# Reordering the prologue of a spectral-mixing and gated-FFN kernel: filter copies, first reads of D and A, and PE filler

## The chip, the cores and the metric

The kernel runs on one core of one Trainium2 chip. The metric is the time of one execution in microseconds of device time. Three runs of the kernel before gave 899.15, 899.78 and 900.06 us; the median is 899.78 us. One further execution was taken with the hardware profiler; it took 901.15 us, of which the profile's span covers 899.4 us.

## What is computed

Eight batches of 3008 x 256 numbers are filtered along the sequence in the frequency domain, and the result goes through a gated feed-forward layer:

```python
X = np.fft.rfft(x, axis=1)                        # x: (8, 3008, 256)
Y = X * (filt_r + 1j * filt_i)[None]              # filters: (1505, 256)
y = np.fft.irfft(Y, n=3008, axis=1).reshape(24064, 256)
gate = np.maximum(y @ w_gate, 0.0)                # 256 x 1536
out = (gate * (y @ w_val)) @ w_out                # 1536 x 256
```

## The kernel before

**Tiling of the transform.** A sequence of 3008 is treated as 94 x 32. Stage A is a DFT over the 94 (matmuls against the table `WA`), stage B a DFT over the 32 (table `F2`), then comes the product with the filters, the inverse of stage B (tables `I2t`, `I2u`) and the inverse of stage A (stage C, table `M1`). Between A and B and between the inverse of B and C the data has to change its layout. For batch 0 the first change is made on chip: `first_a` writes `AS`, and two VectorE transposes (`turn_a`, L292) make `AT`. For batch 1 it goes through HBM: `items_a(1)` makes sixteen items (four slabs c of four pieces j); an item is one float32 matmul (L304) and one eviction (L307), and each finished slab of four is stored to `Abuf` (L310); `load_at` reads it back as `at` in four transfers (L382). The second change goes through HBM for every batch: `inv` stores `Dbuf` (L445) and `load_d` reads `dC` (L471). From batch 2 on the items are made by a different path (`tiled_a`, table `WF`), which the change does not touch.

**Feed-forward blocks.** 24064 rows are cut into 47 blocks of 512. `item_c` makes the input of a block (`yT`) from `dC`; `gv` makes one of twelve pieces of gate and value (weights `WgT`, `WvT`, L510); `o_part` multiplies with `WoT` (L531), one block behind. The main loop runs `gv` and `o_part` and hangs the pieces of the next batches' transforms on numbered steps (`at_step`). The first of these, `fwd(1, 0)` at step 16, is the first reader of `at`.

**The prologue** is everything ahead of the main loop, and its order is written out by hand; each engine and each DMA queue executes in the order in which it is written. Three engines issue transfers: SP, ACT and POOL. POOL's transfers also convert float32 to bfloat16; filters and weights come in that way. An issuing engine waits in place for whatever its transfer needs, and everything written behind that transfer on the same engine waits with it.

The steps of the prologue that matter here, in the order of the code:

- `warm(n)` issues n matmuls on a tile of ones, `junk`, whose result nobody reads; it is filler for PE.
- `load_x(0, ...)` loads batch 0's x into `XF[0]` and `XF[1]` in column quarters of q = 1024 columns.
- `hold_gpsimd(tile)` is a tiny copy on POOL that makes POOL wait until a tile has landed. The first one stands ahead of `load_filters`, which loads the filters in two halves (groups 0 to 11, then 12 to 23), for `Ftr` and `Fti`, for two partition ranges a.
- `place_filter(fi, a, half, copy)` copies 32 partitions of a filter tile to the next 32 (L255). Eight such copies exist; one runs on POOL, seven are transfers on SP's queue.
- `load_x(1, ...)` loads batch 1's x over batch 0's, on SP's queue, when batch 0's stage A has read it.
- `first_b(amid)` runs the six steps i of batch 0's stage B: `fwd(0, i)`, four products, `inv(0, i-2)`, then `amid(i)`, which inserts filler and items of `items_a(1)` into PE's order. Products run on VectorE (L413) or, through a copy `xs` on ACT, on POOL (L411). PSUM has eight banks; `bank` hands them out in the order in which they were given back.
- After `first_b` come the first read of D for block 0 (`load_d(0, 0, 1, ...)`), the second half of the gate and value weights (`load_vg`), further reads of D, `load_o`, the rest of the items with `item_c(0, h)` in between, and `load_at(1, c)`.

The first read of D has two halves e, one on each of the two engines in `engs`. POOL waits for it with a second `hold_gpsimd`, so that the weights' second half starts behind it.

Of the kernel before, what the change touches and what calls it, by code (L numbers as in the profile page):

```python
# [35 lines left out]
def _ap(t, offset_elems, ap_list):  # L36
    return dataclasses.replace(
        t, offset=t.offset + offset_elems, ap=[list(p) for p in ap_list]
    )
# [81 lines left out]
def kernel(  # L121
# [10 lines left out]
    nc = tc.nc  # L132
# [11 lines left out]
    wa_h, fold_h, f2_h, tab_h = _tables()  # L144
# [8 lines left out]
    def bank(name, *shape):  # L153

        i = free.pop(0)
        t = ps.tile([128, *shape], FP32, tag=f"bank{i}", bufs=1, name=name)
        held[id(t)] = i, t
        return t

    def done(t):  # L160
        free.append(held.pop(id(t))[0])
# [7 lines left out]
    XF = [pro.tile([128, NX2 * D], FP32, name=f"XF{c}") for c in range(N2 // NX2)]  # L169
# [3 lines left out]
    WF = consts.tile([128, 4, 32], FP32)  # L173
# [11 lines left out]
    def load_x(b, engs, cols, ms=range(3)):  # L185
        w = NX2 * D
        for c, c0, c1 in cols:
            for m in ms:
                rows = min(32, B * N1 - (b * N1 + 32 * m))
                engs[m % len(engs)].dma_start(XF[c][m:m + 4 * rows - 3:4, c0:c1],  # L190
                              _ap(x, (b * N1 + 32 * m) * N2 * D + c * w + c0,
                                  [[N2 * D, rows], [1, c1 - c0]]))
# [38 lines left out]
    def load_filters():  # L231

        for g0 in (0, H):
            for src, dst in FILT:
                for a in range(2):
                    r, k1, n = a * 64, 1 + 24 * a + g0, H - (2 * a if g0 else 0)
                    nc.gpsimd.dma_start(dst[r:r + 31:2, g0:g0 + n, :],
                                        _ap(src, k1 * D, [[N1 * D, 16], [1, n * D]]))
                    nc.gpsimd.dma_start(dst[r + 1:r + 32:2, g0:g0 + n, :],
                                        _ap(src, (N1 - k1) * D, [[N1 * D, 16], [-D, n], [1, D]]))  # L240
            yield
# [8 lines left out]
    def place_filter(fi, a, half, copy):  # L250

        dst = FILT[fi][1]
        gs = slice(H * half, H * half + H)
        r = a * 64
        copy(dst[r + 32:r + 64, gs, :], dst[r:r + 32, gs, :])  # L255

    def place_nyq():
        for (src, dst), n in zip(FILT, nyq):
            nc.gpsimd.tensor_copy(dst[96:97, NG - 1, :], n)

    def load_vg(c0, c1):
        for (w_hbm, w_sb) in ((moe_w_val, WvT), (moe_w_gate, WgT)):
            nc.gpsimd.dma_start(w_sb[:, :, c0:c1],
                                _ap(w_hbm, c0, [[DFF, 128], [128 * DFF, 2], [1, c1 - c0]]))
# [7 lines left out]
    def hold_gpsimd(tile_):  # L272

        scr = sb.tile([128, 8], FP32, tag="scr", bufs=2)
        nc.gpsimd.tensor_copy(scr[:tile_.shape[0]], tile_)  # L275
# [19 lines left out]
    slabs = []  # L295

    def items_a(b):

        def one(c, j, st):
            if j == 0:  # L300
                st["asb"] = sb.tile([128, NC2 * D], BF16, tag="asb", bufs=4, name="asb")
            psA = bank("psA", 512)
            o = (c * NC2 % NX2) * D + j * 512
            nc.tensor.matmul(psA[0:NROW], WA[:, 128:], XF[c * NC2 // NX2][:, o:o + 512],  # L304
                             start=True, stop=True)
            copy = nc.vector.tensor_copy if c > 1 or (c, j) in ((0, 1), (0, 3)) else nc.scalar.copy
            copy(st["asb"][:NROW, j * 512:(j + 1) * 512], psA[0:NROW])  # L307
            done(psA)
            if j == 3:
                slabs.append(lambda: nc.sync.dma_start(  # L310
                    _ap(Abuf[b], c * NROW * NC2 * D, [[NC2 * D, NROW], [1, NC2 * D]]), st["asb"][:NROW]))
                if c != 1:
                    while slabs:
                        slabs.pop(0)()
        for c in range(N2 // NC2):
            st = {}
            for j in range(NC2 * D // 512):
                yield lambda c=c, j=j, st=st: one(c, j, st)
# [58 lines left out]
    ats = {}  # L377

    def load_at(b, c):
        if c == 0:  # L380
            ats[b] = sb.tile([128, NG, D], BF16, tag="at", bufs=1, name="at")
        nc.gpsimd.dma_start(ats[b][c:c + 125:4],  # L382
                          _ap(Abuf[b], c * NROW * NC2 * D, [[D, 32], [4 * NC2 * D, NG], [1, D]]))

    psXs, tus, dsbs, left = {}, {}, {}, {}
# [81 lines left out]
    def load_d(b, z0=0, z1=NZ, engs=(nc.sync, nc.sync)):  # L467
        for z in range(z0, z1):
            dC = sb.tile([NROW, 8, D], BF16, tag="dC", bufs=6)
            for e in range(2):  # L470
                engs[e].dma_start(dC[48 * e:48 * e + 48],  # L471
                                  _ap(Dbuf[b], (64 * e + 16 * z) * NG * D,
                                      [[D, 48], [48 * D, 8], [1, D]]))
            dCs[b, z] = dC
# [3 lines left out]
    def runs(t, n):  # L478

        o = 0  # L480
        while o < n:
            b, r = divmod(t + o, S)
            n2, n1 = divmod(r, N1)
            w = min(N1 - n1, n - o)
            yield o, b, n2, n1, w
            o += w

    def item_c(k, h):

        if h == 0:  # L490
            yTs[k] = sb.tile([128, 2, W], BF16, tag="yT", bufs=3, name="yT")
        psY = bank("psY", W)
        for (o, b, n2, n1, w) in runs(k * W, W):
            nc.tensor.matmul(psY[:, o:o + w],  # L494
                             dCs[b, n2 // 8][:, n2 % 8, h * 128:(h + 1) * 128], M1[:, n1:n1 + w],
                             start=True, stop=True)
        dst = yTs[k][:, h]
        if h == 0:
            nc.scalar.copy(dst, psY)  # L499
        else:  # L500
            nc.vector.tensor_copy(dst, psY)  # L501
        done(psY)
# [57 lines left out]
    junk = pro.tile([128, 512], BF16, tag="junk", bufs=1)  # L560

    def warm(n, cols=512):

        psJ = bank("psJ", 512)
        for i in range(n):
            nc.tensor.matmul(psJ[:, :cols], junk[:, 0:128], junk[:, :cols], start=True, stop=True)
        done(psJ)

    q = NX2 * D // 4
    both, sp = (nc.sync, nc.scalar), (nc.sync,)  # L570
    nc.sync.dma_start(WA, nc.inline_tensor(wa_h, name="dft_wa").ap())
    load_x(0, both, ((0, 0, q),), range(4))
    nc.vector.memset(junk, 1.0)
    nc.vector.memset(XF[0][:, q:2 * q], 0.0)
    nc.gpsimd.memset(XF[0][:, 2 * q:], 0.0)
    nc.vector.memset(XF[1][:, 0:2 * q], 0.0)
# [5 lines left out]
    for (src, dst) in FILT:  # L582
        nc.vector.memset(dst[64:128, NG - 2:, :], 0.0)
    filters = load_filters()
    hold_gpsimd(XF[1][:, 2 * q - 8:2 * q])
    next(filters)
    load_own_filters()
    next(filters)

    warm(6)  # L590
    for p, s, h in [(p, s, h) for p in range(2) for s in range(2) for h in range(2)]:
        first_a(p, s, h)
    for p, h in ((2, 0), (3, 0), (2, 1), (3, 1)):
# [9 lines left out]
    for i in range(6):  # L603
        warm(2)
    place_filter(1, 0, 0, nc.gpsimd.tensor_copy)
    for a in range(2):
        place_filter(0, a, 0, nc.sync.dma_start)
    place_filter(1, 1, 0, nc.sync.dma_start)
    load_x(1, sp, ((0, 0, 2 * q),))
    for fi in range(2):  # L610
        for a in range(2):
            place_filter(fi, a, 1, nc.sync.dma_start)
    load_x(1, sp, ((0, 2 * q, 4 * q),))

    early = items_a(1)

    def amid(i):
        if i == 3:
            place_nyq()
            load_vg(0, DFF // 2)  # L620
        if i == 3:
            load_x(1, sp, ((1, 0, 4 * q),))
        if i < 4:
            warm(2)
        for _ in range((0, 0, 0, 0, 1, 1, 1)[i]):
            next(early)()

    first_b(amid)
    load_d(0, 0, 1, (nc.scalar, nc.scalar))
    hold_gpsimd(dCs[0, 0][:, 7, D - 8:])  # L630
    load_vg(DFF // 2, DFF)
    load_d(0, 1, 2, (nc.gpsimd, nc.gpsimd))
    load_o()
    load_d(0, 2, 4, (nc.gpsimd, nc.gpsimd))
    nc.sync.dma_start(WF, nc.inline_tensor(fold_h, name="dft_fold").ap())
    for i, f in enumerate(early):
        f()
        if i == 9:
            for h in range(2):
                item_c(0, h)  # L640
    for c in range(4):
        load_at(1, c)
    prologue.close()
    fs = ctx.enter_context(tc.tile_pool(name="fs", bufs=2))
    XP = []
# [80 lines left out]
```

## Time and profile before

| what | value |
|---|---|
| median of three runs | 899.78 us (899.15 to 900.06) |
| profiled execution | 901.15 us, span 899.4 us |
| PE busy | 877.4 us, 98% of the span |
| VectorE, ACT, POOL busy | 573.0, 495.3, 379.0 us |
| mean granted PE clock | 0.989 |
| first `gv` matmul | 63.26 us after the span's start |
| first matmul on `at` | 83.32 us |

Times inside the profile are counted from the start of the span. In the views of DMA queues, q0 is POOL's queue, q1 is SP's and q10 is ACT's. A row of the view of windows gives the length of the window, each engine's busy time in it with the number of instructions in brackets, the PE clock that was granted (1.00 is full, 0.50 half), the share of the window in which the 16 DMA engines held packets (it can exceed 1, when several packets are under way at one engine), and GB/s. The two rows of the table on `gv` and `at` bracket the region that the change touches: the main loop behind it is the same code.

### The profile page before, as it was taken

How to read it: one execution, taken by the hardware profiler on the slowest of the kernel's cores; microseconds unless marked ns; L12 is line 12 of the kernel's file. 1: busy time of each engine (PE TensorE's matmuls, PEld its weight loads, DVE VectorE, ACT ScalarE, POOL GpSimd, SP SyncE). 2: the span in 40 equal slices, each digit the busy share in tenths (PEclk: the TensorE clock that was granted, in tenths of full speed). 3: DMA queues.
4: the chain of work that ended last, by engine and by line, in shares of the span. 5: the costliest groups of instructions: out<-in, count | busy, mean ns of one | idle time of the engine just before them, and what ended most of it. 6: DMA issues, size and time to landing. Idle time of an engine off the chain costs nothing.

```text
span 899.4 us, 19131 instructions
## 1 busy us (share of the span) xinstructions
PE 877.4 (98%) x7177; PEld 508.6 (57%) x7177; DVE 573.0 (64%) x868; ACT 495.3 (55%) x887; POOL 379.0 (42%) x378
## 2 busy tenths in 40 slices
PE   8788999999999999999999999999999999999997
PEld 3234564556555665566655566556655566666665
DVE  3646775667665776657766677656766577655553
ACT  5524665555655556555655565655565555555552
POOL 5624498118680386514773167701868000000001
PEclk9889999999999999999999999999999999999999
DMA  8897448443465344663355433753346512231111
GB/s 235 236 207 163 118 126 175 102 117 109 135 158 124 92 132 120 140 140 108 97 149 144 114 101 104 181 124 92 108 139 154 118 32 81 78 77 36 36 33 51
DMA packets 105810, 107.59 MB, mean 120 GB/s; under 512 B 20295, under 2 KB 89703, under 8 KB 105142
## 3 DMA queue, kind: packets, MB, share of 16 engines
q1 hardware_dynamic: 81126, 76.30, 32.9%
q0 software_dynamic: 23440, 29.16, 13.8%
q8 instruction: 56, 0.92, 0.4%
q10 hardware_dynamic: 1152, 0.92, 0.4%
q14 instruction: 36, 0.29, 0.1%
HBM read 60.55 MB, written 48.23 MB: 121 GB/s over the span
## 4 chain that ended last, share of the span: by engine, by line
PE 88%; DMA 7%; DVE 1%; issue 1%; SPq 1%; POOL 1%; ACT 0%; DVEq 0%; POOLq 0%; ACTq 0%
PE psV L510 26%; PE psO L531 26%; PE psG L510 25%; PE psF L354 3%; PE psD L434 2%; PE psY L494 2%; DMA at<-Abuf 2%; PE psX L397 2%; DMA dC<-Dbuf 2%; PE psA L283 1%; DVE AT L292 1%; DMA WvT<-in_moe_w_val_dram 1%; DMA Ftr<-Ftr 1%; DMA Abuf<-asb 1%; PE psA L304 1%
## 5 line engine op out<-in xcount | busy, mean ns | idle before, releaser
L515 DVE SCALAR_TENSOR_TENSOR prod<-psG,vsb 128x512 bf16<-128x512 f32 x564 | 388.7, 690 | 262.5 <-ACT vsb L513 254.9
L513 ACT CAST vsb<-psV 128x512 bf16<-128x512 f32 x564 | 332.1, 589 | 271.1 <-PE psV L510 228.4
L510 PE MATMUL psV<-yT,WvT 128*128 128x512 bf16 x1128 | 337.4, 380 | 0.6 <-DVE yT L501 0.6
L531 PE MATMUL psO<-WoT,prod 128*128 128x256 bf16 x2256 | 336.9, 273 | 0.0
L510 PE MATMUL psG<-yT,WgT 128*128 128x512 bf16 x1128 | 336.0, 380 | 0.0
L531 PEld LDWEIGHTS <-prod 128*128 128x128 bf16 x2256 | 221.0, 98 | 143.9 <-issue 0.8
L510 PEld LDWEIGHTS <-WgT 128*128 128x128 bf16 x1128 | 110.2, 98 | 135.0 <-issue 2.4
L510 PEld LDWEIGHTS <-WvT 128*128 128x128 bf16 x1128 | 98.6, 98 | 41.3 <-issue 30.1
L275 POOL CAST scr<-prod 128x8 f32<-128x8 bf16 x24 | 4.6, 190 | 248.3 <-DVE prod L515 248.3
L555 POOL DMA_DIRECT2D out_dram<-osb x5 | 2.6, 531 | 195.7 <-ACT osb L544 195.7
L413 DVE TENSOR_TENSOR tt<-psX,Ftr 128x512 bf16<-128x512 f32 x96 | 64.9, 680 | 6.2 <-PE psX L397 2.7
L544 ACT COPY osb<-psO 128x512 f32<-128x512 f32 x92 | 54.0, 586 | 26.6 <-PE psO L531 25.4
L340 POOL TENSOR_TENSOR fold<-XP 128x1024 f32<-128x1024 f32 x24 | 56.5, 2354 | 21.0 <-PE psF L354 18.9
L413 DVE TENSOR_TENSOR uu<-psX,Fti 128x512 bf16<-128x512 f32 x88 | 59.8, 679 | 2.4 <-DMA Fti<-Fti 2.4
L442 ACT CAST dsb<-psD 128x512 bf16<-128x512 f32 x94 | 50.5, 590 | 16.1 <-PE psD L434 16.1
L327 POOL DMA_DIRECT2D XP<-in_x_dram x96 | 57.7, 603 | 2.8 <-PE psY L494 1.5
L341 POOL TENSOR_TENSOR XP<-XP 128x1024 f32<-128x1024 f32 x24 | 56.3, 2348 | 2.0
L361 DVE CAST asb<-psF 128x512 bf16<-128x512 f32 x48 | 30.9, 686 | 18.5 <-PE psF L354 18.5
L361 ACT CAST asb<-psF 128x512 bf16<-128x512 f32 x48 | 25.8, 589 | 30.5 <-PE psF L354 30.5
L499 ACT CAST yT<-psY 128x512 bf16<-128x512 f32 x47 | 27.6, 586 | 25.7 <-PE psY L494 25.5
L494 PE MATMUL psY<-M,dC 96*128 96x94 bf16 (+18 forms) x604 | 38.1, 200 | 2.7 <-DMA dC<-Dbuf 2.7
L494 PEld LDWEIGHTS <-dC 96*128 96x128 bf16 x604 | 34.7, 98 | 7.1 <-issue 2.7
(75 smaller groups left out, 505.5 us busy)
## 6 DMA issues: line engine op xcount, KB each, us to landing
XP<-in_x_dram POOLq DMA_DIRECT2D x48, 256.0 KB, 6.1
Dbuf<-dsb SPq DMA_DIRECT2D x23, 512.0 KB
dC<-Dbuf SPq DMA_DIRECT2D x56, 192.0 KB
XP<-in_x_dram POOLq DMA_DIRECT2D x96, 96.0 KB, 2.7
Abuf<-asb SPq DMA_DIRECT2D x96, 96.0 KB
at<-Abuf SPq DMA_DIRECT2D x24, 384.0 KB
out_dram<-osb SPq DMA_DIRECT2D x69, 94.0 KB
XF<-in_x_dram SPq DMA_DIRECT2D x15, 256.0 KB
```

The costliest lines, as they stand in the source:

```text
L327: nc.gpsimd.dma_start(xp[r:r + 24, 0:4:2, :], _ap(x, (b * N1 * N2 + o) * D, [[N2 * D, 24], [47 * N2 * D, 2], [1, 512]]))
L340: tt(t, xp[:, 0:2], xp[:, 2:4], op=ALU.add)
L341: tt(xp[:, 2:4], xp[:, 0:2], xp[:, 2:4], op=ALU.subtract)
L361: copy(asf[:, :, q, :], banks[q])
L413: nc.vector.tensor_tensor(p, psX, filt, op=ALU.mult)
L442: copy(dsb[:, a, o:o + 2, :], psD[a])
L494: nc.tensor.matmul(psY[:, o:o + w], dCs[b, n2 // 8][:, n2 % 8, h * 128:(h + 1) * 128], M1[:, n1:n1 + w], start=True, stop=True)
L510: nc.tensor.matmul(pt[:, :W], w[:, h, ft * 128:(ft + 1) * 128], yt[:, h, :], start=(h == 0), stop=(h == 1))
L513: nc.scalar.copy(vsb, psV[:, :W])
L515: nc.vector.scalar_tensor_tensor(prod, in0=psG[:, :W], scalar=0.0, in1=vsb, op0=ALU.max, op1=ALU.mult)
L531: nc.tensor.matmul(psO[:, t % 2], prods[ft][:, t * 128:(t + 1) * 128], WoT[:, ft, :], start=(ft == 0), stop=(ft == NFT - 1))
L544: copy(osb[:, t0 % 2:t % 2 + 1], psO[:, t0 % 2:t % 2 + 1])
```

## The change

The edits, all in the prologue:

1. The filler ahead of `first_a` is 18 matmuls of 256 columns in place of 6 of 512, and the 256 columns of `junk` that these read are set by POOL; VectorE sets the other 256.
2. The first `hold_gpsimd` waits for the last columns of `XF[0]` in place of columns in the first half of `XF[1]`, which is the transfer group behind.
3. All seven filter copies on SP's queue are issued first, and then all of batch 1's x, without copies in between; the last third of x is no longer issued in `amid(3)`.
4. `amid` inserts 1, 2, 2 and 2 items at i = 3, 4, 5, 6 (before: 1 at 4, 5 and 6), and three filler matmuls at i = 0, 1, 2 (before: two at 0 to 3). The first half of the gate and value weights is issued at i = 5 in place of 3.
5. The first read of D has one half on SP's queue and the other on ACT's (before: both on ACT's), and the four stores to `Abuf` are issued behind it and behind all items, where before each went out when its slab was done.
6. `item_c(0, h)` stands ahead of the last two items in place of the last three.
7. `load_at` is issued on SP's queue in place of POOL's, and the table `WF` behind it.

```diff
@@ items_a
             if j == 3:
                 slabs.append(lambda: nc.sync.dma_start(... Abuf[b] <- asb ...))
-                if c != 1:
-                    while slabs:
-                        slabs.pop(0)()
@@ load_at
-        nc.gpsimd.dma_start(ats[b][c:c + 125:4],
+        nc.sync.dma_start(ats[b][c:c + 125:4],
@@ prologue
-    nc.vector.memset(junk, 1.0)
+    nc.gpsimd.memset(junk[:, 0:256], 1.0)
+    nc.vector.memset(junk[:, 256:], 1.0)
...
-    hold_gpsimd(XF[1][:, 2 * q - 8:2 * q])
+    hold_gpsimd(XF[0][:, 4 * q - 8:])
...
-    warm(6)
+    warm(18, 256)
...
     place_filter(1, 0, 0, nc.gpsimd.tensor_copy)
-    for a in range(2):
-        place_filter(0, a, 0, nc.sync.dma_start)
-    place_filter(1, 1, 0, nc.sync.dma_start)
-    load_x(1, sp, ((0, 0, 2 * q),))
-    for fi in range(2):
-        for a in range(2):
-            place_filter(fi, a, 1, nc.sync.dma_start)
-    load_x(1, sp, ((0, 2 * q, 4 * q),))
+    for fi, a, half in ((0, 0, 0), (0, 1, 0), (1, 1, 0), (0, 0, 1), (0, 1, 1), (1, 0, 1), (1, 1, 1)):
+        place_filter(fi, a, half, nc.sync.dma_start)
+    load_x(1, sp, ((0, 0, 2 * q), (0, 2 * q, 4 * q), (1, 0, 4 * q)))
@@ amid
         if i == 3:
             place_nyq()
+        if i == 5:
             load_vg(0, DFF // 2)
-        if i == 3:
-            load_x(1, sp, ((1, 0, 4 * q),))
-        if i < 4:
-            warm(2)
-        for _ in range((0, 0, 0, 0, 1, 1, 1)[i]):
+        if i < 3:
+            warm(3)
+        for _ in range((0, 0, 0, 1, 2, 2, 2)[i]):
             next(early)()
@@ behind first_b
-    load_d(0, 0, 1, (nc.scalar, nc.scalar))
+    load_d(0, 0, 1, (nc.sync, nc.scalar))
...
-    nc.sync.dma_start(WF, nc.inline_tensor(fold_h, name="dft_fold").ap())
     for i, f in enumerate(early):
         f()
-        if i == 9:
+        if i == 6:
             for h in range(2):
                 item_c(0, h)
+    for store in slabs:
+        store()
     for c in range(4):
         load_at(1, c)
+    nc.sync.dma_start(WF, nc.inline_tensor(fold_h, name="dft_fold").ap())
```

## The prediction

> **What bounds the kernel now.** I read the page first: 98% busy PE means that only waits of PE, and PE running at a low clock, can be won. So next comes the list of PE's waits over the whole span; its longest rows, with the span ahead of them:
>
> ```profile
> span 899.4 us, 19131 instructions
> PE psD L434 <- DVE uu L413: 4.3, 1, 4.3
> PE psY L494 <- DMA dC<-Dbuf: 2.7, 2, 1.5
> PE psX L397 <- DMA at<-Abuf: 2.6, 2, 2.1
> PE psA L304 <- ACT asb L307: 1.5, 1, 1.5
> ```
>
> The first three name the three handovers of the prologue: filters, first read of D, first read of A. Of the second and third, 1.1 and 2.1 us lie in the prologue. Third view, the chain that ended last, in order of time (start, length):
>
> ```profile
> 26.59 6.91 DMA Ftr<-Ftr
> 34.01 2.57 DMA Fti<-Fti
> 47.69 6.08 DMA Abuf<-asb
> 53.81 3.27 DMA dC<-Dbuf
> 57.66 7.21 DMA WvT<-in_moe_w_val_dram
> 74.54 8.65 DMA at<-Abuf
> ```
>
> From 26 to 83 us the end is carried by transfers, one after another. Fourth, windows around these waits:
>
> ```profile
> core 0: us, PE busy (x) PEld busy (x) DVE busy (x) ACT busy (x) POOL busy (x), PEclk, DMA share, GB/s
> 30.00:33.20 3.20, 2.40 (x38) 1.06 (x36) 1.49 (x3) 3.02 (x7) 2.92 (x4) 1.00 0.52 112
> 33.20:37.45 4.25, 0.00 (x0) 0.00 (x1) 1.44 (x3) 1.27 (x3) 1.24 (x2) 0.84 0.71 190
> 57.20:63.20 6.00, 5.99 (x18) 2.51 (x19) 2.06 (x3) 0.59 (x1) 5.73 (x9) 0.50 0.90 192
> 68.00:72.00 4.00, 4.00 (x25) 1.89 (x23) 3.26 (x5) 2.81 (x6) 1.91 (x3) 1.00 1.34 252
> 83.30:87.10 3.80, 3.78 (x19) 1.76 (x20) 1.98 (x3) 1.18 (x3) 0.00 (x0) 0.58 0.00 0
> ```
>
> Two things: a wait is paid twice, because PE then runs at half clock (0.50 after the read of D costs 3.0 us of 6.0; 0.58 after the read of A costs 1.6 of 3.8). And outside the gaps the DMA engines are full (0.90 to 1.34), so what is pulled forward pushes something back.
>
> **Filler and stage A of batch 0.** Before, filler runs 1.45 to 4.19 us, PE idles 0.96 until x lands, and the first evictions stand 1.71 us apart, later 0.86: two matmuls at half clock. Filler now has 4608 columns in place of 3072, 2.74 x 1.5 = 4.1 us, and starts after a POOL memset, at about 1.05; it closes the gap. Worth 0 to 1.7 us. Its cover is x, which lands at 5.0 anyway. Against it: the first hold on POOL was released at 12.24 by one group of x (0.79 MB; 303 GB/s in the window 5 to 12, so 2.6 us a group); now it is released a group earlier, near 9.65, and the filter loads run beside the last group. In the window 24 to 31, with both queues busy, SP's queue moved 1.10 MB and POOL's 0.41, that is 157 and 59 GB/s. The 0.6 MB of x still to come then take 3.9 in place of 2.0 us, landing near 16.7 where the eleventh matmul started at 15.3. Bounds for stage A as a whole: -1.5 (clock gained, no interference) to +3 (interference, and the clock lost in that wait); I take +1.0, nearest to the two-queue row.
>
> The Trainium skill (TensorE: Matmul & The Clock Gate, "What's actually happening") says that the clock follows free-running windows of about 3.4 us of activity. The trace agrees in kind: 0.96 us of idleness ahead of x kept the clock low, and the low spell behind the read of D lasted 6.0 us. By the page the longer filler would contain a whole window only in some executions, so its gain would be a matter of phase; the sum does not count any.
>
> **Filters, then x.** SP's copies of Fti's second half were issued at 32.79, after a wait for loads that POOL issued by 23.6: they shared the engines with 0.79 MB of batch 1's x. POOL's queue alone moved 0.55 MB in the window 15 to 19, 138 GB/s; the 0.41 MB of the window 24 to 31 would then need 3.0 us, and with the copies between them 4: loads landed at 28 in place of 32.8. Being released 2.6 us earlier at the hold could bring up to 2.6 more, but the share is 0.91 to 0.99 there, so I count 0. The copies are used 2.2 us after the last issue (34.5 to 36.7), so at about 32, when VectorE gets there (27.8 + 4.3): the 4.3 us wait goes. (It reached PE through a bank: `inv(0, 2)` needs the one that the product with Fti gives back.)
>
> Late next is x, now behind all copies: 28 + 2 issues x 0.86 + 3 issues x 0.61 + 2.2 = 33.5. The item in `amid(3)` needs it, and behind it in PE's order stand `fwd(4)` and all else. `inv(0, 1)` ends at 32 + 1.0 = 33.0, so PE waits 0.5. Then one item 0.88 (18 matmuls in 7.96 us, two to an item), twice [fwd 0.4, inv 0.45, two items 1.75], then inv, two items, inv 2.7: 42.3. Eviction and issue add 0.8: the last store of D's first input goes out at 43.1, before at 46.40. Gain 3.3, filler being equal in number of columns (9 and 8 pieces).
>
> **Store and first read of D.** Before, issue to landing took 7.0 (46.40 to 53.40), beside 0.79 MB of weights; these are now issued about as late relative to it, so I take 6.7. The read took 3.8 (53.40 to 57.2); SP's half now has the A stores right behind, ACT's half competes with them: 3.8 to 5.5, I take 4.4. On SP the four A stores and A's reads wait behind this read; nobody needs them before `fwd(1, 0)`. On ACT one eviction waits behind it (before, four banks were held, the 1.5 us row). D lands at 54.2, 3.0 earlier; bounds 0 and 5.5.
>
> **From D to the main loop.** Before 6.06: 0.5 for `item_c`, three items 2.6, 3.0 lost to the clock. After: 0.5 + 1.7 + 2.3 (mean of the two spells above) = 4.5. Gain 1.5.
>
> **A's reads.** They leave POOL's queue, where they came last (issued 68.7 to 75.2, landed 83.3), and go out behind the last A store, about 3 us into the main loop. The first reader comes 18.0 after the loop's start (63.26 to 81.25), so the wait of 2.1 and its clock loss of 1.6 go: 3.7.
>
> **What is late next: the weights.** The rest of POOL's queue starts when D lands. Before, relative to that, the second half of WgT landed at 10.3, WoT at 14.6 and 17.0. Needed, with the loop at 4.5: 10.2 for WgT, 16.7 and 18.0 for WoT. A's 1.54 MB now run beside them; at 230 GB/s (between 199 and 252 of the rows) that can push them by 0 to 6.7. I take 3 on WoT: 2.0 late, and 0.5 of clock: 2.5. Bounds 0 and 6.7 - 1.0 + 1.6 = 7.3.
>
> The Trainium skill (DMA: Bandwidth & Descriptors, "Issuing engines are not separate DMA queues") says that transfers issued from different engines run on the same 16 DMA engines, so that another issuer saves only issue time. The shares above 0.9 on both queues agree with it. By that rule alone the 2.5 above would be near its upper bound, and the change would gain about 1.
>
> **Sum.** -3.0 - 1.5 - 3.7 + 2.5 = -5.7. Against the profiled execution's 901.15 (span 899.4, 1.75 around it) that makes 895.4; the median of the runs lies 1.37 lower, and I carry the same difference to the median: 899.8 - 5.7 = 894.1. The main loop is the same code and cannot give back more than its waits. The measurement can tell 0.2%, 1.8 us.
>
> **Rivals.**
> - *Everything in time.* The early hold does bring the filters 2.6 sooner and the weights are not pushed: -5.7 - 2.5 - 2.6 = -10.8, 889. For it: 0.52 and 0.71 of DMA share from 30 to 37 us are room. Against it: 0.9 and more elsewhere.
> - *x late.* x lands 4 us later than reckoned; PE stands in `amid(3)` with everything behind it: -1.7, 898.1. For it: x is issued at 30 in place of 21.9. Against: 33.5 is only 0.5 beyond PE's own pace.
> - *Waits change names.* Whatever is won ahead of D is lost to weights: 899.8.
> - *Slower: the DMA engines are the bound.* The bytes until D lands are the same; with the engines full D lands no earlier (0), and A's reads push WoT by the whole 7.3: 0 - 1.5 - 3.7 + 7.3 = +2.1, 901.9, and up to 904 if stage A also loses clock. For it: shares of 0.9 to 1.34. Against: the gaps at 30 to 37 and 54 to 57 us (0.53). It decides from the point where waits for weights exceed 7.0 us with D no earlier.
>
> **How the numbers follow.** Forecast 0.55, everything in time 0.14, x late 0.10 (half of it within 1.8 us), names 0.07, slower 0.14. Faster 0.55 + 0.14 + 0.05 = 0.74, same 0.12, slower 0.14. The range reaches from 888.5 (most of the first rival) to 900.2 (names and x late inside), leaving out the slower case and the fastest tail.
>
> **What would show it.** Right: no PE wait of 4 us between 30 and 38; SP's last filter copies issued near 28; first read of D landed near 54; first `gv` near 58.7; no wait for `at`, but one or two for WoT or WgT in the first two blocks. Wrong: a wait for x at L304 of over 2 us; stage A's last transfer holding PE near 16 by more than 2; D landing at 57 or later; PE waiting more than 5 us for weights.

## The result, and the profile after

The changed kernel takes 896.1 us (median of 20 runs), the kernel before 898.9 us in 20 runs. The ratio is 0.9968 with a 95% interval of 0.9955 to 0.9981: faster by 2.9 us, between 1.7 and 4.0. The forecast was 5.7 us. So it went the way that was foretold and brought half of what was reckoned; the table and the traces below say how much of that half stands where it was looked for. The profiled execution took 896.65 us, with a span of 894.8 us.

PE's waits in the changed kernel (us in total, times, longest):

```profile
core 0 of [0], span 894.8 us
PE psY L491 <- DMA dC<-Dbuf: 5.7, 2, 4.8
PE psX L394 <- DMA at<-Abuf: 2.6, 2, 1.7
PE psA L304 <- DMA XF<-in_x_dram: 2.3, 1, 2.3
PE psO L528 <- DMA WoT<-in_moe_w_out_dram: 1.4, 1, 1.4
```

The row of 4.3 us for the filters is gone. In its place stand x at L304 with 2.3, and `WoT` with 1.4, which no row of before had. The wait for `at` is still there. The first wait for D is longer, since PE now reaches it with fewer items left. The chain that ended last, in order of time (start, length):

```profile
29.35 4.16 DMA XF<-in_x_dram
33.65 1.99 PE psA L304 x2
45.41 6.20 DMA Dbuf<-AS
51.79 3.63 DMA dC<-Dbuf
60.86 7.59 DMA Abuf<-asb
68.51 13.20 DMA at<-Abuf
```

Transfers still carry it, in the old order, with x in place of the filters. Two matmuls at L304 need 1.99 us: a low clock. The windows show it:

```profile
core 0: us, PE busy (x) PEld busy (x) DVE busy (x) ACT busy (x) POOL busy (x), PEclk, DMA share, GB/s
31.40:33.65 2.25, 0.00 (x1) 0.03 (x1) 1.16 (x2) 1.76 (x4) 2.25 (x3) 0.99 0.83 269
33.65:37.00 3.35, 3.35 (x27) 1.28 (x27) 0.71 (x2) 1.17 (x2) 1.11 (x3) 0.50 0.99 301
55.50:60.90 5.40, 5.35 (x18) 2.41 (x20) 2.06 (x3) 0.59 (x1) 5.08 (x8) 0.50 0.93 214
65.00:70.00 5.00, 5.00 (x29) 2.23 (x28) 3.61 (x6) 3.48 (x7) 3.62 (x3) 1.00 1.24 253
```

PE stands still for 2.26 us and then runs 3.35 us at 0.50, which costs 1.7 us more. Behind D the same happens as before, 5.4 us at 0.50. The DMA share is 0.83 to 1.24 in these rows. The steps side by side:

| step | before | predicted | after |
|---|---|---|---|
| first transpose of batch 0 starts | 18.17 | 19.2 | 17.43 |
| last filter copies issued on SP | 32.79 | 28 | 26.80 |
| batch 1's x first used | no wait | 33.5, wait 0.5 | 33.65, wait 2.26 |
| last store of D's first input issued | 46.40 | 43.1 | 45.41 |
| D landed | 57.2 | 54.2 | 55.55 |
| first `gv` matmul | 63.26 | 58.7 | 59.90 |
| wait for `WoT` | none | 2.0 | 1.44 |
| wait for `at` | 2.07 | none | 1.72 |
| first matmul on `at` | 83.32 | not given | 81.76 |

VectorE makes 564 products (`prod`) in the main loop, and their starts are milestones. From the first to the 25th it is 32.8 us before and 32.7 after: what came 3.4 us earlier at the first `gv` is neither added to nor lost over that stretch. At the 25th the changed kernel is 3.25 us ahead (94.45 against 97.70), and from the 100th to the last both take 676.2 us. But from the last product to the end of the span it is 11.10 us before and 10.04 after. The prediction has no term for this 1.06 us; run e2 shows which edit brings it.

### The profile page after: what moved, and what is told of

The parts are those of the page before. It is cut to its first block, busy times and chain, and to the rows that moved or that the text cites. A ratio compares the mean times of both kernels' runs of the same rounds, so it can differ in the third digit from the quotient of the medians.

```text
span 894.8 us, 19034 instructions
## 1 busy us (share of the span) xinstructions
PE 868.0 (97%) x7069; PEld 508.7 (57%) x7190; DVE 573.0 (64%) x868; ACT 494.8 (55%) x887; POOL 376.2 (42%) x375
## 4 chain that ended last, share of the span: by engine, by line
PE 85%; DMA 7%; DVE 3%; ACT 2%; SPq 1%; issue 1%; POOL 0%; ACTq 0%; DVEq 0%
PE psG L507 25%; PE psO L528 25%; PE psV L507 23%; PE psF L351 3%; DMA at<-Abuf 3%; PE psD L431 2%; PE psY L491 2%; PE psX L394 2%; DVE prod L512 2%; DMA dC<-Dbuf 2%; ACT vsb L510 1%; PE psA L304 1%; DMA XF<-in_x_dram 1%; DMA Abuf<-asb 1%; DVE AT L292 1%
## 5 line engine op out<-in xcount | busy, mean ns | idle before, releaser
L507 PE MATMUL psG<-yT,WgT 128*128 128x512 bf16 x1107 | 330.8, 379 | 5.3
L507 PE MATMUL psV<-yT,WvT 128*128 128x512 bf16 x1030 | 316.0, 380 | 0.6 <-DVE yT L498 0.6
L541 ACT COPY osb<-psO 128x512 f32<-128x512 f32 x92 | 53.9, 586 | 25.9 <-PE psO L528 24.6
L410 DVE TENSOR_TENSOR uu<-psX,Fti 128x512 bf16<-128x512 f32 x88 | 59.9, 681 | 0.0
L491 PEld LDWEIGHTS <-dC 96*128 96x128 bf16 x604 | 34.7, 98 | 10.1 <-DMA dC<-Dbuf 5.6
```

The lines of the kernel that those rows point to most:

```text
L410: nc.vector.tensor_tensor(p, psX, filt, op=ALU.mult)
L491: nc.tensor.matmul(psY[:, o:o + w], dCs[b, n2 // 8][:, n2 % 8, h * 128:(h + 1) * 128], M1[:, n1:n1 + w], start=True, stop=True)
L507: nc.tensor.matmul(pt[:, :W], w[:, h, ft * 128:(ft + 1) * 128], yt[:, h, :], start=(h == 0), stop=(h == 1))
L541: copy(osb[:, t0 % 2:t % 2 + 1], psO[:, t0 % 2:t % 2 + 1])
```

## The experiments

Two theories stood against each other. **A:** the DMA engines are full behind D's read, so that only the bytes ahead of a transfer decide when it lands, and ahead of D the new wait for x costs its length and the clock behind it. **Rival:** it is the queues, the place of a transfer in SP's or POOL's order, that decide. All times are medians. The kernel before ran beside each; the ratio is to it, and the changed kernel's own is 0.9968. Down to e12 the edits are on the changed kernel, in the last three rows on the kernel before. Differences are of medians unless the ratio is named; the medians come from different occasions, on which the kernel before had 898.6 to 899.2, so the ratio is the surer measure and is given too where the two differ; the intervals of e3, e4, e5, e6 and e10 lie wholly below the changed kernel's.

| run | edit in a word | us | ratio (95%) |
|---|---|---|---|
| e1_late_hold | POOL's hold a group later | 895.9 | 0.9961 (0.9945 to 0.9978) |
| e3_fill_for_x | filler in place of an item at i = 3 | 893.5 | 0.9931 (0.9916 to 0.9947) |
| e2_at_on_pool | A's reads on POOL | 897.0 | 0.9973 (0.9958 to 0.9989) |
| e4_d_behind_at | later D reads behind A's | 893.3 | 0.9922 (0.9903 to 0.9942) |
| e6_fill_before_c | both, and filler ahead of D | 891.9 | 0.9932 (0.9916 to 0.9947) |
| e10_weights_early | both, weights at i = 3 | 891.1 | 0.9912 (0.9894 to 0.993) |
| e5_fill_and_d_behind | e3 and e4 together | 891.0 | 0.9919 (0.9905 to 0.9934) |
| e7_a_store_first | one A store ahead of D's read | 895.2 | 0.9965 (0.9947 to 0.9983) |
| e12_d_read_on_act | D's read on ACT alone | 894.0 | 0.9943 (0.9923 to 0.9963) |
| e9_filler_alone | before, edit 1 | 898.7 | 0.9994 (0.9981 to 1.0007) |
| e8_copies_first_alone | before, edit 3 | 897.8 | 0.9989 (0.9977 to 1.0002) |
| e11_copies_and_regrouping | before, edits 3, 4, 6 | 897.9 | 0.9985 (0.9972 to 0.9997) |

### The new wait for x: e3 and e1

```diff
-        if i < 3:
-            warm(3)
-        for _ in range((0, 0, 0, 1, 2, 2, 2)[i]):
+        if i < 4:
+            warm((3, 3, 3, 8)[i])
+        for _ in range((0, 0, 0, 0, 3, 2, 2)[i]):
```

> The changed kernel with no item at i = 3 (eight filler matmuls there instead) and three items at i = 4: PE does not stand in front of batch 1's x. Theory A: the wait for x cost 2.3 us and 1.7 us more through the clock (0.50 from 33.65 to 37.0); with filler the clock stays at 1.00, the last store of D's first input goes out at 43.3 in place of 45.4, D lands at 53.6 in place of 55.6, and the time falls by 1.5 to 2 us, to 894.4. Rival B: stores to D and first weights are bound by the DMA engines anyway (share about 1.0 from 42 to 51 us), D lands at 55.5 as before, and the time is the same within 0.5 us.

893.5 us, 2.6 under the changed kernel. The same window as above, of this kernel:

```profile
33.65:37.00 3.35, 3.35 (x31) 1.34 (x30) 2.34 (x5) 2.26 (x6) 1.78 (x3) 1.00 0.90 308
```

The clock is 1.00 where it was 0.50, the last store of D's first input goes out at 42.65 in place of 45.41, and D lands at 53.25 in place of 55.55. The wait for x and the clock behind it had thus cost D 2.3 us, where 1.35 were missing from the forecast (54.2). By the ratios the run is 3.3 under the changed kernel.

```diff
-    hold_gpsimd(XF[0][:, 4 * q - 8:])
+    hold_gpsimd(XF[1][:, 2 * q - 8:2 * q])
```

> The changed kernel with the first hold put back: POOL's filter loads start when the first half of batch 0's XF[1] has landed, as before. Theory A: in the changed kernel POOL's ninth load waited 2.6 us for the first one, which took 7 us beside batch 0's x, so the early hold won only 0.05 us for the second half of the filters (ninth load at 17.20, before at 17.25). Then SP's last filter copies go out at 26.8 within 0.5, batch 1's x lands at 33.5 within 0.5, and the time is that of the changed kernel within 0.1% (895.5 to 897). Rival: the early hold is what made the filters 6 us earlier in part; then the copies go out at 29.4, x lands at 36, and the time is 2 to 3 us above the changed kernel's.

The copies are issued at 28.30 in place of 26.80, where theory A had expected no shift, and D lands at 57.43 in place of 55.55, yet the time is that of the changed kernel. The early hold is worth 1.5 us at the copies and nothing that the runs can tell in the end; their intervals are some 1.5 us wide to each side. In the two traces the lead is lost late: 1.55 us at the 25th product (94.45 against 96.00), none at the 100th (208.49 against 208.01), since the changed kernel waits 0.9 us for D and 0.8 for `at` in between. Why POOL's release, 3.0 us earlier (10.25 against 13.24), brings the copies only 1.5 is seen in POOL's timeline of the changed kernel (start, length, instruction, idle time ahead of it and its releaser):

```profile
14.01 0.61 POOL L239 DMA_DIRECT2D Fti<-in_filt_i_dram  x1
17.20 0.52 POOL L245 DMA_DIRECT2D Ftr<-in_filt_r_dram  x1 [2.59 <-DMA Ftr<-in_filt_r_dram]
```

The filter loads start at 10.25, but the ninth stands idle for 2.59 us behind the first, which ran beside the last of x and landed at 16.64, after 6.4 us. In the trace's records the first eight loads carry eight different semaphores, and the ninth carries that of the first again and waits for it. It is issued at 17.20, in e1 at 17.54.

### Behind D: e2, e4, e6 and e10

```diff
-        nc.sync.dma_start(ats[b][c:c + 125:4],
+        nc.gpsimd.dma_start(ats[b][c:c + 125:4],
```

> The changed kernel with A's reads back on POOL's queue, behind all weights. Theory A: behind the landing of D the 16 DMA engines are full and the same bytes decide; A lands 26 us after D whoever issues it (before 26.1, changed kernel 26.2), so the first matmul on it stays at 81.8 within 1; WoT then lands 17 us after D in place of 20 and its wait of 1.4 us goes, without a gain in time, because the wait for A grows by as much. Time within 1 us of the changed kernel. Rival: SP's queue brought A forward; then the first matmul on A is 2 us or more later and the time is 2 to 4 us above the changed kernel's.

897.0 us, within the interval of the changed kernel. PE's waits, and the first matmul on `at`:

```profile
PE psX L394 <- DMA at<-Abuf: 3.3, 2, 2.0
PE psA L304 <- DMA XF<-in_x_dram: 2.1, 1, 2.1
```

```profile
80.13 0.41 PE L394 MATMUL psX<-at,F 64*64 64x256 bf16 x8 [2.03 <-DMA at<-Abuf]
```

There is no wait for `WoT`, and `at` comes 24.6 us after D, earlier than the 26.2 on SP's queue. SP's queue had not brought A forward; it only put the wait on another name. The rival falls. That A came 1.6 us earlier from POOL is more than theory A allowed for, and not explained. The Trainium skill says this in DMA: Bandwidth & Descriptors, "Issuing engines are not separate DMA queues": transfers of all issuers end on the same 16 engines. This run agrees with it, 897.0 against 896.1 us, and so do the bytes between D's landing and A's in the view of the DMA queues, first the kernel before (57 to 83 us), then the changed one (55.5 to 82):

```profile
DMA packets 3283, 5.54 MB, mean 213 GB/s; under 512 B 272, under 2 KB 2320, under 8 KB 3280
```

```profile
DMA packets 6132, 5.63 MB, mean 212 GB/s; under 512 B 300, under 2 KB 5548, under 8 KB 6129
```

The issuer does count in one place, the end of the program. From the end of POOL's last issue to the end of the span it takes 6.33 or 6.34 us in all five traces with A's four reads on POOL (the kernel before, e2, e8, e9, e11; 187 transfers issued by POOL). It takes 5.27 or 5.28 in four of the five with 183 transfers (5.41 in e7), and 4.84 to 4.93 in the four with 179 (e4, e5, e6, e10). What POOL does in that time the profile doesn't show. So 1.06 us of the change's gain come from edit 7, behind the last product; e2 gives them back (0.9 by the medians), though its interval alone could not tell this from nothing.

If the bytes decide, then a read that is needed late has to go behind A:

```diff
-    load_d(0, 2, 4, (nc.gpsimd, nc.gpsimd))
...
     for c in range(4):
         load_at(1, c)
+    load_d(0, 2, 4)
```

> The changed kernel with the last two reads of D (four transfers, 0.79 MB, first needed by block 2's input near 90 us) taken from POOL's queue and issued on SP's, behind A's reads. Theory A, engines full: A lands 3 us earlier (23 us after D in place of 26), WoT up to 1 us earlier; the wait for A of 1.7 us goes, and the time falls by 1.5 to 2.5 us, to 894.2. Rival: A's landing is set by its own chain (last store to A at 60.9, landing 68.5, then 13 us for its read), and taking 0.79 MB away does not change it: same time within 0.5 us. A third way: block 2's input then waits for D and gives the gain back, a wait of over 1 us at psY near 92 us.

893.3 us, 2.8 under the changed kernel, by the ratios 4.1. Neither `at` nor `WoT` is waited for; the row of the first matmul on `at` has no bracket behind it:

```profile
81.02 0.41 PE L394 MATMUL psX<-at,F 64*64 64x256 bf16 x8
```

From the loop's first product to its 25th it takes 29.5 us in place of 32.7. In this execution x was waited for 3.4 us and D landed at 57.85, later than in the changed kernel: the gain lies behind D, where the theory puts it, but for 0.35 us at the end of the program (four transfers fewer on POOL).

Run e6 is the two edits above together, and 24 filler matmuls ahead of `item_c(0)` (`warm(24)`), so that the clock would stay up across the wait for D.

> e5_fill_and_d_behind with 24 more filler matmuls ahead of item_c(0), where PE otherwise stands about 5 us for D and then runs 5 to 6 us at half clock. Theory A, engines full behind D: the loop starts up to 2.5 us earlier at full clock, but WgT and WoT land at the same distance from D as before (10 and 18 us), so PE waits for them and most of it is given back: 0 to 1 us gained on e5, waits for WgT, WoT or the second read of D appear or grow. Rival B, the clock is what bounds the start of the loop: 2 to 3 us gained on e5, no new waits. If the filler outlasts the wait for D, up to 0.5 us lost.

891.9 us against 891.0 without that filler (e5), with intervals that overlap: no gain. The clock was 1.00 there and the loop started at 56.0 in place of 58.5, but from its first product to its 25th it took 33.4 us, in e5 29.6. PE's waits:

```profile
PE psG L507 <- DMA WgT<-in_moe_w_gate_dram: 2.4, 1, 2.4
PE psX L394 <- DMA at<-Abuf: 1.4, 1, 1.4
PE psY L491 <- DMA dC<-Dbuf: 1.2, 1, 1.2
```

The first, with a spell of half clock behind it (64.9 to 68.3), lies ahead of the 25th product and takes back what was won; the other two come behind 95 us.

Run e10 is e5 with the first half of the weights issued at i = 3 in place of 5.

> e5_fill_and_d_behind with the first half of the gate and value weights issued at i = 3, as the kernel before did, in place of i = 5 (about 38 in place of 41 us). Theory A, engines full: the weights' 0.79 MB only change places with x and the stores to D; the last store of D's input takes 1 us less than its 6.5 us but goes out later or equal, D lands within 1 us of 54.1, time within 1 us of 891.0. Rival: the late weights are what delays D's input; D lands 1.5 to 2 us earlier and the time is 1 to 2 us lower.

891.1 us, as e5. Asking earlier for the same bytes is worth nothing that can be seen; A holds here too. (In its profile `WgT` cost 1.3 us and `WoT` 1.0, where e5 shows 0.2 for `WoT`.)

### Both edits together: e5

> The edits of e3_fill_for_x and e4_d_behind_at together on the changed kernel. Theory: they take different waits (in front of D; behind D), so their gains add: loop start 2.8 earlier, and 3.2 less from the loop's start to the end of its second block, against the changed kernel. Time 896.1 - 2.7 - 3.0 = 890.4, within 1.2. Rival: both relieve the same 16 engines, so that the earlier D only meets weights that are late by as much; then the time stays at 892.5 to 893.5, that of either alone.

891.0 us, 7.6 under the kernel before and 5.1 under the changed one. It beats both kernels. By the medians the two gains of 2.6 and 2.8 add up; by the ratios they are 3.3, 4.1 and together 4.4, each with an interval of about 1.5 us to each side, so the times do not settle it. The traces show both gains in their places: the loop's first product is at 60.26 in place of 61.73, and from there to the 25th it takes 29.6 us in place of 32.7, as in e4. PE's waits of this run:

```profile
PE psY L491 <- DMA dC<-Dbuf: 5.9, 2, 5.1
PE psX L394 <- DMA at<-Abuf: 0.2, 1, 0.2
PE psO L528 <- DMA WoT<-in_moe_w_out_dram: 0.2, 1, 0.2
```

What is left is the first read of D, with 5.1 us.

### Stores and the read of D: e7 and e12

```diff
+    slabs.pop(0)()
     load_d(0, 0, 1, (nc.sync, nc.scalar))
```

> The changed kernel with one of the four A stores (0.38 MB) issued ahead of D's first read, as before, the other three behind it. Theory A, engines full: 0.38 MB at 230 GB/s are 1.7 us, so D lands 0.5 to 1.7 us later relative to the last store of D's input (10.1 us from that issue to landing in the changed kernel), and most of it comes back when A lands: time 0 to 1 us above the changed kernel. Rival: stores behind the read cost D nothing and one ahead of it costs the whole 1.7 plus its completion: time 2 us or more above.

895.2 us, as the changed kernel. From the last store's issue to D's landing it is 10.1 us (46.47 to 56.55), and 10.1 in the changed kernel too: one A store ahead of the read costs D nothing that can be seen. Theory A had expected 0.5 to 1.7 us there, so it misses in this detail.

```diff
-    load_d(0, 0, 1, (nc.sync, nc.scalar))
+    load_d(0, 0, 1, (nc.scalar, nc.scalar))
```

> The changed kernel with both halves of D's first read on ACT's queue, as before. Theory P (issuers are not resources where the DMA engines are full): time equal to the changed kernel's within 1.5 us, the wait for an ACT-held bank at L304 back with 1 to 2 us, and the read itself within 0.5 us of 3.85. Rival R (the split is what brought D's read in): the read takes over 4.5 us or is issued over 1 us later, and the time is 2 us or more over the changed kernel's.

894.0 us. Issue to landing is 10.3 us (45.64 to 55.92), so splitting the read over two queues did not bring it in, and the rival falls. The theory was wrong in a detail: only one eviction stood behind the read on ACT, and PE did not wait for its bank. The run is 2.1 us under the changed kernel by the medians, but the intervals overlap. In its trace SP, not blocked by D's read, issues the first A store at 46.20, where the changed kernel issues it at 52.08:

```profile
46.20 0.82 SPq L310 DMA_DIRECT2D Abuf<-asb  x1
```

and `WoT` is no longer waited for. That the split costs something is likely and not settled: e7 has that early store too and is no faster than the changed kernel.

### Parts of the change alone: e9, e8 and e11

Run e9 is the kernel before with edit 1 (18 filler matmuls of 256 columns, `junk` set by two engines).

> The kernel before with the filler edit alone: 18 matmuls of 256 columns from 1.1 us on, the first 256 columns of junk set by POOL. Theory: the first evictions of stage A stand 0.86 apart in place of 1.71, and the transposes start at 17.4 in place of 18.2, no earlier, because x of the second group (landing at 9.7) is the next thing to wait for; but the filters' wait behind it is set by POOL's loads, which do not move, so it grows by what stage A gains and nothing is left: the time is that of before within 1 us. Rival: stage A's 0.7 us go through to the end: time 0.7 to 1.7 us under before.

898.7 us, as before. The first evictions stand 0.86 us apart in place of 1.71 and the transposes start at 17.55 in place of 18.17, but the filters are still waited for at `psD` (2.6 us in two waits, where the theory had the wait grow), and D lands at 56.64. The interval reaches from 1.7 us under before to 0.6 over it, so a gain of stage A's 0.7 us is not ruled out.

Run e8 is the kernel before with edit 3 (all seven copies first, all of x behind).

> The kernel before with this one part of the change: all seven filter copies on SP's queue ahead of batch 1's x, everything else as before (one item each at i = 4, 5, 6, D's first read on ACT's queue, A's reads on POOL's, the late hold). Theory: the wait of 4.3 us for the filters goes and with it 2 to 2.6 us of half clock; x lands at 35 and the first item at i = 4 then waits 0 to 1.5 us; the last store of D's input goes out at 42 to 44 in place of 46.4; D lands 2 to 4 us earlier, and the time is 2 to 4 us under the kernel before, no less than the whole change gives. Rival: the filters' wait is only exchanged for x's: the last store goes out at 45.5 to 46.5 and the time is that of before within 1 us, so the change's 2.9 us come from its other parts.

897.8 us, by the ratio 1.0 under before and perhaps nothing (the interval reaches 1.0002); 2 to 4 were expected, so it misses. D did land at 54.57, 2.6 earlier than before and earlier than in the changed kernel, and in this one execution the lead grew to 4.5 us at the 25th product (93.17 against 97.70). The medians show little of it: the profiled execution of before lies 2.3 us above the median of its kernel and that of e8 1.4 below, so one trace against another overstates the gain here. PE's waits show where this kernel still loses:

```profile
PE psX L397 <- DMA at<-Abuf: 3.2, 2, 2.3
PE psA L304 <- ACT asb L307: 3.0, 1, 3.0
PE psY L494 <- DMA dC<-Dbuf: 1.3, 2, 0.9
```

The items behind D's read wait 3.0 us for banks that ACT holds, since ACT stands at both halves of the read. That is the row of 1.5 us of before, twice as long.

Run e11 adds to e8 the regrouping, edits 4 and 6.

> The kernel before, with edit 3 (all copies first, batch 1's x behind) and edits 4 and 6 (one, two, two and two items at i = 3 to 6, filler at i = 0 to 2, the weights' first half at i = 5, item_c ahead of the last two items). Left as before: the filler ahead of stage A, the hold, both halves of D's first read on ACT's queue, the stores to Abuf as slabs are done, A's reads on POOL's queue. Theory P (the parts measured alone add up: the filler, the hold, the store order and A's issuer are each worth nothing, and the copies alone 1.0 us, so the regrouping carries the other 2): ratio 0.996 to 0.998, 1.8 to 3.6 us under the kernel before, equal to the changed kernel; a wait for x at L304 of about 2 us, and D landed near 55.5. Rival Q (the regrouping is worth nothing, and the rest comes from the stores behind the first read of D together with A's reads behind them): 0 to 1.3 us under the kernel before, a wait for a bank held by ACT of over 2 us at L304, D landed at 57 or later.

897.9 us, 1.3 under before by the ratio (0.3 to 2.5) and 0.7 by the medians: between the two theories, and nearer to Q by the time, though the interval reaches into P's range. The wait for ACT's bank is gone, but x is waited for 2.4 us, and behind it the clock stays low for longer than in the changed kernel:

```profile
35.60:42.30 6.70, 6.70 (x50) 2.51 (x53) 2.57 (x4) 2.62 (x5) 1.95 (x4) 0.58 0.95 325
```

6.7 us at a mean of 0.58 are 2.8 us lost, against 1.7 in the changed kernel. D lands at 59.64, where P had 55.5, and later than before, so P misses there. Of what Q wanted, that the stores and A's reads bring the rest, one part is shown: the 1.06 us at the end of the program, which this kernel, with A's reads on POOL, does not have. The remainder is not shown, because this run has POOL's late hold as well, and x is later by 1.7 us (35.39 against 33.65; with the late hold alone, in e1, 35.04).

## Why the prediction was right or wrong

**Right:** what is won ahead of the main loop, and where. The filters' wait goes (copies at 26.80, predicted 28), x is needed at 33.65 (33.5), D comes earlier, the way from D to the loop is 4.35 us (4.5), `WoT` lands 20.2 us after D (20.0) and is waited for 1.44 us (2.0). The early hold was counted at nothing; e1 shows 1.5 us for it at the copies and nothing that can be told in the time. The rival that the DMA engines are the bound has the mechanism behind D right, but D did come 1.65 us earlier, so its sign was wrong.

**Mis-sized, first: the wait for x, at 0.5 with no clock behind it.** It measured 2.26, and 1.7 of clock. PE's own pace was wrong: it stood there at 31.4 and not at 33.0 (the copies alone came 1.2 earlier than reckoned), while x came when it was reckoned. So it was not the length of the wait that made D late, but the clock, which the sum had at nothing: the prediction's opening rule, a wait is paid twice, was applied to the waits that go and not to the one that comes. From x to the last store of D's first input it took 11.8 us in place of 9.6, and 1.7 of the difference is the clock; the store went out at 45.41 in place of 43.1. From there to D's landing it took 10.1 in place of 11.1, an error of the other sign. So D landed 1.65 us earlier in place of 3.0, and 1.0 us of agreement in this number is luck. The prediction itself had named a wait of over 2 us at L304 as a sign against it. Run e3 shows the price: with filler in that place the store goes at 42.65 and D lands at 53.25.

**Mis-sized, second: A's reads on SP's queue, at 3.7.** `at` is still waited for, 1.72 us in place of 2.07; of the 3.7 only the 1.6 of clock behind it went, and 0.35. The clock stood at 1.00 behind this wait, in e8 too, which waited 2.35 us, but not in e2, which waited 2.03 (in order, the changed kernel, e8, e2):

```profile
81.70:85.00 3.30, 3.19 (x25) 1.90 (x27) 2.26 (x4) 1.66 (x3) 0.00 (x0) 1.00 0.00 0
80.48:85.00 4.52, 4.51 (x34) 2.66 (x35) 3.54 (x6) 2.25 (x4) 0.00 (x0) 1.00 0.05 10
81.03:84.44 3.41, 3.41 (x13) 1.52 (x11) 1.53 (x3) 1.76 (x3) 0.00 (x0) 0.50 0.01 3
```

So that the 1.6 went is not shown to be the change's doing; it can be luck. Against it stand `WoT` with 1.44 us (2.5 predicted, with its clock) and half a microsecond of low clock that now falls into the loop (59.9 to 60.9). Term by term, from the first `gv` on: -0.35 - 1.6 + 1.44 + 0.5 = 0, and the 25th product says -0.1; predicted was -3.7 + 2.5 = -1.2. The reason is in e2 and e4: about the same bytes (5.5 to 5.7 MB) go through the same engines at 212 to 219 GB/s, whoever issues them; A's wait went only when something else went behind it (e4). The prediction quoted the rule that says so, worked out that by it the change would gain about 1, and sided with the place in the queue.

**Wrong in sign, without effect: stage A of batch 0, at +1.0.** It gained 0.7: the last group of x did not hold PE. By e9 what is won there is worth nothing that the runs can tell, which fits a sum that left it out.

**Not foreseen: the end of the program.** Of the measured 2.9 us, 1.06 come from the four transfers fewer on POOL and lie behind the last product (e2). What the change brings where the prediction looked is then about 1.8, with the interval's 1.2 to each side, against the forecast 5.7, and that the whole came to half of the forecast is in part luck.

**What stays open.** The spans of the two profiles differ by 4.6 us: 3.25 at the 25th product, 0.3 from there to the 100th, 1.06 at the end. The medians differ by 2.8, so about 1.8 of it belongs to the two executions and not to the change. The stretch from the 25th product to the 100th, with later waits for D and `at`, takes 112.0 to 114.9 us in the fourteen traces, and no run explains that. And the rest of the 2.9 us can't be shared out among the edits. Edit 1, the hold and the place of the A stores are each nothing that can be told by e9, e1 and e7, A's issuer is nothing that can be told ahead of the program's end, the copies with the regrouping bring only 1.3 (e11), and how much a given execution loses to the clock behind x (1.7 here, 2.8 in e11) weighs as much as any of them.

The phases of low clock fit the Trainium skill, TensorE: Matmul & The Clock Gate, "What's actually happening", which gives windows of about 3.4 us. The traces show such windows: in the first 100 us of all fourteen, behind the first rise of the clock, every spell of low clock lasts 3.41, 6.83 or 10.24 us, one, two or three times the same length. The spell behind the read of D in the kernel before, which the prediction put at 6.0 us from a window set by hand, lasts 6.83 (56.61 to 63.44). The first row is the changed kernel's spell behind x, the other two are the two halves of the one in e11:

```profile
33.60:37.01 3.41, 3.36 (x27) 1.32 (x27) 0.72 (x2) 1.17 (x2) 1.16 (x3) 0.50 0.99 303
34.35:37.76 3.41, 2.37 (x14) 0.78 (x18) 0.19 (x1) 0.78 (x2) 2.05 (x4) 0.50 1.01 298
37.76:41.17 3.41, 3.41 (x23) 1.49 (x16) 2.26 (x4) 1.90 (x4) 1.15 (x1) 0.50 0.94 346
```

In the changed kernel x came 0.05 us into the window, PE was busy for 3.36 of its 3.41 us, and the clock rose at its end. In e11 x came 1.04 into it, PE was busy for 2.37, and the clock stayed low for one more. In these traces no low spell ended behind a window with PE busy for less than 94%, and none went on behind one with more than 86%. So the price of one wait is a matter of where it falls in the windows as well as of its length: behind a wait of 1.84 us for x (e7) the spell was 6.83 us, behind one of 2.55 (e12) it was 3.41.

## What to carry to other kernels

A wait that a change brings is to be priced like one that it takes away: its length and the low clock behind it; some filler ahead of it, in place of useful work that can stand behind, can be worth as much as the change itself (2.6 us here, 3.3 by the ratios). Where the DMA engines were full, another issuer (e2) or an earlier issue (e10) gained nothing that could be told at the wait, it only gave the wait another name; a transfer that is needed late is better put behind the one that is waited for (2.8 us here, 4.1 by the ratios). When a part of a change is priced, look at the end of the program too: here POOL's four transfers were worth more there than at the wait that they were moved for. An issuer that is released earlier only helps if its transfers can then land; look whether a later one waits for the landing of the first. And two traces are two executions: hold their difference against the medians before it is called the change's.

## What the hardware showed that was not expected

- POOL's ninth filter load carries the semaphore of the first again and waits for its landing: 2.59 us of idle time in the changed kernel.
- The end of the program takes longer the more transfers POOL has issued: 6.3 us behind its last issue with 187, 5.3 with 183, 4.8 to 4.9 with 179. With 179 SP's last work ends within 0.04 us of POOL's, so SP may set the end there.
- The granted clock fell and rose on a grid of 3.41 us; low spells were one, two or three of these long.
- With two queues busy the first filter load took 6.4 us beside x, and behind D a store of 384 KB to `Abuf` took 7.59 us and a read of 384 KB 13.20.
- The same reads came 1.6 us earlier from POOL's queue (24.6 us after D) than from SP's (26.2), though they were written behind the weights there.
- A wait for x of 2.3 us cost 1.7 us of clock in one kernel, and one of 2.4 us cost 2.8 in another.
